# Rounding the last two weight pieces together, one slot later, in a fused attention and MLP kernel

## The chip, the core and the metric

The kernel runs on one core of a Trainium2 chip. The metric is device time in microseconds (us): the median of three runs is 1388.27 us, from 1384.64 to 1389.68. Five engines work side by side, each through its own instructions in order: TensorE (PE; its weight loads are shown as PEld), VectorE (DVE), ScalarE (ACT), GpSimd (POOL) and SyncE (SP, which here only starts transfers). They wait for each other through semaphores.

## The reference

Eight batches of eight heads attend over 576 positions of 64 channels, with a threshold on the scores. The result goes through a two-layer MLP with an exact gelu.

```python
scores = scale * np.matmul(q, k.transpose(0, 1, 3, 2))
thresh = np.max(scores, axis=-1, keepdims=True) - tau
scores = np.where(scores >= thresh, scores, -1000000000.0)
attn = np.exp(scores - np.max(scores, axis=-1, keepdims=True))
attn = attn / (np.sum(attn, axis=-1, keepdims=True) + 1e-09)
x = np.matmul(attn, v)          # then (B,H,S,D) -> (B*S, H*D): 4608 x 512
h = x @ w_in                    # 512 x 2048
out = (0.5 * h * (1.0 + erf(h / sqrt(2)))) @ w_out      # 2048 x 512
```

q, k, v and the result are 32-bit. The weights `moe_w_in` and `moe_w_out` arrive as 64-bit floats and have to be rounded to 32 bits on the core.

## The kernel before, in words

**Slots.** Two heads of a batch make a pair; there are 32 pairs. A pair's queries are cut into five chunks (`SLOTS`): four of 128 queries for each head, and one that holds the last 64 of both heads. One chunk of one pair is a slot, and the main loop (L832) goes over slots n = 0, 1, 2, ... The first batch's four pairs ("early", p = 0 to 3) take the first twenty slots: chunks 0 and 1 of each pair in n = 0 to 7, chunks 2, 3 and 4 in n = 8 to 19. So n = 17, 18 and 19 are chunks 2, 3 and 4 of pair 3, and n = 20 (`BATCH`) is the first slot of pair 4, where the later way of working begins.

**One slot.** PE computes the scores (L353). DVE takes the negated row maximum (L365), POOL the threshold (L366), ACT the exponential (L368), and DVE masks it by the threshold and sums each row (L384, "the mask" below). In an early slot the division and the turning of the probabilities are one matmul: DVE takes the reciprocal of the sums (L395), ACT scales an identity matrix by it (`diag`, L398), and PE multiplies the probabilities with that diagonal (L295), one slot later. ACT copies the turned tile from PSUM (L303, L314); for the last pair's chunk 4 DVE does so (L307, L319, `copy` at L305). After that, PE weighs v with them (L470).

**Between.** Into the same PE order `fill` puts steps of the MLP, block by block of 256 tokens: the first layer (L545) and the second (L559). How many steps a slot gets is planned by a cost per matmul (`goal`, `owed`), and a step is only placed once the weight pieces it needs are rounded in program order. Up to slot n = 19 the first layer's results are copied out ungelued (L512) and held; at n = 20 six of them go through gelu at once (L518). The last ten blocks go through a different scheme with fewer products (L679) at the end.

**Rounding the weights.** The weights are 32 pieces of 128 x 512 values: 16 of w_in, then 16 of w_out. `load_piece` brings a piece in two copies, `raw` and `shifted`, the second three bytes on. Pieces with an even number land in two buffers of the pool `xg` (seven buffers, shared with the MLP's input blocks `x_blk`). Pieces with an odd number land in a part of `turned_p` (L142), which the attention does not need before n = 20. Four pieces are loaded ahead: the load of piece k is issued when piece k - 4 is done. `conversions` rounds a piece with four DVE instructions and one of ACT: L168 (exponent bits), L169 on ACT (scaling them), L174 (mantissa bits), L176 (sign, needs L169) and L178 (product, the 32-bit value). It works one piece ahead: L168 and L169 of the next piece come before L174 of the one in hand.

`conversions` is a generator that yields a cost after each step, 2100 ns for a piece in all. The loop calls `convert(ns)` once a slot, after the mask and ahead of `diagonal` (the reciprocal and the diagonal): nothing at n = 0, 2000 ns at n = 1 and 2, 3800 ns up to n = 18, and from n = 19 on without limit (L896). Up to n = 18 that is 64,800 ns, enough for 30.9 pieces.

At n = 20 POOL clears parts of `pd_tail` and `turned_p` (L885), and the later slots write `turned_p` with DVE transposes (L431).

Of the kernel before, what the change touches and what calls it, by code (L numbers as in the profile page):

```python
# [18 lines left out]
def kernel(  # L19
# [82 lines left out]
    for t in sums:  # L102
# [17 lines left out]
    pieces = [(w_in_sb[c][:, f:f + PIECE], moe_w_in[c * P:(c + 1) * P, f:f + PIECE])  # L120
              for f in range(0, d_ff, PIECE) for c in range(N_DM)]
    pieces += [(w_out_sb[j][:, f:f + PIECE], moe_w_out[j * P:(j + 1) * P, f:f + PIECE])
               for j in range(N_DF) for f in range(0, d_model, PIECE)]
    wide = moe_w_in.dtype != FP32
    raws = []
    loaded = [0]
    converted = [0]

    def load_piece(eng=nc.gpsimd):
        if loaded[0] == len(pieces):  # L130
            return
        dst, src = pieces[loaded[0]]
        loaded[0] += 1
        if not wide:
            nc.sync.dma_start(dst, src)
            converted[0] += 1
            load_piece()
            return
        k = loaded[0] - 1
        if k % 2:  # L140

            room = pd[k // 2 % 2].bitcast(U32)  # L142
            raw, shifted = room[:, 0:2 * PIECE], room[:, 2 * PIECE:4 * PIECE]
        else:
            raw, shifted = (xg.tile([P, 2 * PIECE], U32, tag="x", name=s) for s in ("raw", "shifted"))
        eng.dma_start(raw, src.bitcast(U32))
        n = 8 * PIECE - 4
        eng.dma_start(shifted.bitcast(U8)[:, 0:n], src.bitcast(U8)[:, 3:3 + n])
        raws.append((dst, raw, shifted))

    def conversions():

        vec = nc.vector
        ahead = None  # L160
        while raws or ahead:
            piece = None
            if raws:
                dst, raw, shifted = raws.pop(0)
                hi = raw.rearrange("p (f w) -> p f w", w=2)[:, :, 1]
                top = shifted.rearrange("p (f w) -> p f w", w=2)[:, :, 0]
                power = gp.tile([P, PIECE], U32, tag="g", name="power")
                vec.tensor_scalar(power, hi, 0x7FF00000, None, op0=ALU.bitwise_and)  # L168
                nc.scalar.activation(power, power, AF.Relu, bias=rebias, scale=8.0)  # L169
                piece = dst, hi, top, dst.bitcast(U32), power  # L170
                yield 340
            if ahead:
                dst, hi, top, mant, power = ahead
                vec.tensor_scalar(mant, top, 0x0FFFFFFF, 0x10000000, op0=ALU.bitwise_and, op1=ALU.bitwise_or)  # L174
                yield 340
                vec.scalar_tensor_tensor(power, hi, 0x80000000, power, op0=ALU.bitwise_and, op1=ALU.bitwise_or)  # L176
                yield 720
                vec.scalar_tensor_tensor(dst, mant, 2.0 ** -28, power.bitcast(FP32), op0=ALU.mult, op1=ALU.mult)  # L178
                load_piece()
                converted[0] += 1  # L180
                yield 700
            ahead = piece
# [3 lines left out]
    def convert(ns):  # L186

        if conv["steps"] is None:
            conv["steps"] = conversions()
        conv["debt"] += ns  # L190
        while conv["debt"] > 0:
            took = next(conv["steps"], None)
            if took is None:
                return
            conv["debt"] -= took
# [600 lines left out]
    for _ in range(2):  # L796
        load_piece(nc.sync)
# [34 lines left out]
    for n in range(len(slots) + WEIGH + 1):  # L832
# [40 lines left out]
        if p < HP - 1 and i == 0:  # L873
            turn_qk_early(p + 1)
            if p == 0:
                load_early(3)
                load_v_early(2)
                load_v_early(3)
            if p < 2:
                load_piece()  # L880
# [70 lines left out]
```

## Time and profile before

| | |
|---|---|
| median of three runs | 1388.27 us (1384.64 to 1389.68) |
| profiled execution | 1389.68 us, of which the span of instructions is 1387.9 us |
| busy, share of the span | PE 98%, PEld 70%, DVE 64%, ACT 46%, POOL 31% |
| mean granted PE clock | 0.996 of full speed |
| slot n = 18, first maximum to reciprocal (DVE) | 135.96 to 143.66 us |
| slot n = 19, maximum to reciprocal (DVE) | 143.57 to 147.77 us |

Times in rows are us from the span's start. A timeline row has the start, the duration, the engine, the line, the operation with its output and inputs by name, the count of instructions that follow each other, and in brackets the idle time of the engine just before with what released it. A matmul of 32-bit numbers stands as two records, so "x20" is ten matmuls. The ends of matmuls are modelled, and rows can overlap by a little.

### The profile page before, as it was taken

The numbers are of one execution on the slowest core, as the hardware profiler recorded it, in microseconds if no ns is written. First come the engines' busy times: TensorE is split into PE (matmuls) and PEld (weight loads), VectorE is DVE, ScalarE is ACT, GpSimd is POOL, SyncE is SP. The second block draws the span as 40 slices with busy tenths as digits, with TensorE's granted clock in tenths as the row PEclk, the third lists the DMA queues.
The fourth block names the chain that finished last, engine by engine and source line by source line (L and its number), as shares of the span: only waits on it lengthen the run. The fifth ranks groups of instructions, "written<-read, shape, count | busy, mean of one in ns | idle before, by whom it ended". The sixth has DMA issues, their size and how long they took to land.

```text
span 1387.9 us, 20217 instructions
## 1 busy us (share of the span) xinstructions
PE 1361.0 (98%) x6728; PEld 968.8 (70%) x6728; DVE 892.8 (64%) x1738; ACT 640.1 (46%) x1161; POOL 434.4 (31%) x895
## 2 busy tenths in 40 slices
PE   8898999999999999999999999999999999999999
PEld 6676557467466466466476475588888888888887
DVE  5988777788888888888888888764142232241330
ACT  6766627447457458348367356241141240330420
POOL 4453254455555555554554551100000000000000
PEclk9999999999999999999999999999999999999999
DMA  8988266567777788787788776500000001001000
GB/s 274 279 296 275 56 150 160 130 160 175 161 168 182 156 189 179 157 197 176 157 199 177 162 181 129 116 0 8 23 1 23 23 1 46 16 0 53 8 9 23
DMA packets 215206, 169.19 MB, mean 122 GB/s; under 512 B 114288, under 2 KB 199600, under 8 KB 215104
## 3 DMA queue, kind: packets, MB, share of 16 engines
q1 hardware_dynamic: 191184, 112.84, 36.3%
q0 software_dynamic: 23488, 54.77, 12.9%
q8 instruction: 55, 0.90, 0.3%
q14 instruction: 47, 0.39, 0.1%
q10 hardware_dynamic: 432, 0.30, 0.1%
HBM read 72.73 MB, written 12.52 MB: 61 GB/s over the span
## 4 chain that ended last, share of the span: by engine, by line
PE 91%; DVE 5%; ACT 2%; issue 1%; DMA 1%; POOL 0%; DVEq 0%; ACTq 0%; POOLq 0%
PE bank L679 35%; PE o_ps L559 16%; PE hT L545 15%; PE sc L353 12%; PE xT L470 10%; DVE p L384 1%; DVE power L176 1%; PE tr L295 1%; ACT p L368 1%; PE tr L266 1%; DMA raw<-in_moe_w_out_dram 1%; ACT diag L398 1%; DVE power L168 1%; DVE w_out L178 1%; DVE w_in L178 1%
## 5 line engine op out<-in xcount | busy, mean ns | idle before, releaser
L368 ACT ACTIVATE p<-sc,nmx 128x576 f32<-128x576 f32 x288 | 201.9, 738 | 267.6 <-DVE nmx L365 267.4
L384 DVE SCALAR_TENSOR_TENSOR p<-sc,thr,p 128x576 f32<-128x576 f32 x288 | 225.3, 816 | 68.8 <-ACT p L368 67.3
L365 DVE TENSOR_REDUCE nmx<-sc 128x1 f32<-128x576 f32 x288 | 205.4, 750 | 65.8 <-PE sc L353 64.9
L545 PE MATMUL hT<-x,w_in 128*128 128x256 f32 x1024 | 241.1, 385 | 0.0
L559 PE MATMUL o_ps<-w_out,g 128*128 128x512 f32 x512 | 236.7, 603 | 0.0
L545 PEld LDWEIGHTS hT<-x,w_in 128*128 128x128 f32 x1024 | 189.5, 190 | 49.2 <-issue 23.5
L366 POOL TENSOR_SCALAR thr<-nmx,tau_eff 128x1 f32<-128x1 f32 x288 | 85.2, 296 | 393.3 <-DVE nmx L365 392.5
L559 PEld LDWEIGHTS o_ps<-w_out,g 128*128 128x128 f32 x512 | 93.0, 189 | 110.2 <-issue 108.6
L470 PE MATMUL xT<-pT,v 128*64 128x256 f32 (+1 forms) x1280 | 163.9, 409 | 0.4 <-issue 0.4
L353 PE MATMUL sc<-kT,qT 64*128 64x288 f32 x960 | 157.0, 431 | 2.0 <-DVE p L384 1.9
L431 DVE STREAM_TRANSPOSE turned_p<-p 128x1152 f32<-128x1152 f32 x112 | 154.4, 1379 | 3.9
L353 PEld LDWEIGHTS sc<-kT,qT 64*128 64x128 f32 x960 | 89.5, 187 | 75.0 <-issue 63.8
L470 PEld LDWEIGHTS xT<-pT,v 128*64 128x64 f32 x1280 | 89.0, 137 | 72.8 <-issue 14.0
L679 PE MATMUL bank<-x,w_in 128*128 128x256 f32 x480 | 116.7, 379 | 0.0
L679 PE MATMUL bank<-w_out,unit 128*128 128x256 f32 x520 | 115.5, 379 | 0.0
L223 POOL DMA_DIRECT2D v<-in_v_dram x208 | 111.2, 538 | 4.4 <-issue 2.4
L679 PEld LDWEIGHTS bank<-w_out,unit 128*128 128x128 f32 x520 | 98.8, 190 | 13.4
L679 PEld LDWEIGHTS bank<-x,w_in 128*128 128x128 f32 x480 | 91.2, 190 | 12.8 <-issue 0.5
L679 PE MATMUL bank<-v,unit 128*128 128x256 f32 x320 | 82.1, 379 | 0.0
L214 POOL DMA_DIRECT2D q<-in_q_dram x104 | 70.9, 687 | 9.8 <-issue 8.9
L679 PE MATMUL bank<-unit,turned_p 128*128 128x256 f32 x320 | 73.1, 379 | 0.0
L531 ACT ACT_TABLE_LOAD x56 | 71.8, 1283 | 1.0
(156 smaller groups left out, 1492.9 us busy)
## 6 DMA issues: line engine op xcount, KB each, us to landing
pT<-turned_p SPq DMA_DIRECT2D x448, 160.0 KB, 3.6
pT<-pd_tail SPq DMA_DIRECT2D x112, 80.0 KB, 3.1
q<-in_q_dram POOLq DMA_DIRECT2D x104, 72.0 KB, 3.3
k<-in_k_dram POOLq DMA_DIRECT2D x104, 72.0 KB, 3.2
inv<-turned SPq DMA_DIRECT2D x56, 128.0 KB, 3.9
v<-in_v_dram POOLq DMA_DIRECT2D x156, 40.0 KB, 3.2
x<-x SPq DMA_DIRECT2D x10, 512.0 KB, 4.8
raw<-in_moe_w_out_dram POOLq DMA_DIRECT2D x8, 512.0 KB, 4.1
```

Of the source, the lines that this page charges most:

```text
L223: eng.dma_start(t[r:P:4, e, 0:n, :], rows[:, r * KR:r * KR + n, :])
L353: nc.tensor.matmul(sc[e][:, h, 0:HALF], lhsT=lhsT, rhs=s["kT"][rows, at:at + HALF], start=True, stop=True)
L365: nc.vector.tensor_reduce(nmx[:, e:e + 1], sc, axis=AXIS.XY, op=ALU.max, negate=True)
L366: nc.gpsimd.tensor_scalar(thr[:, e:e + 1], nmx[:, e:e + 1], -1.0, tau_eff, op0=ALU.mult, op1=ALU.subtract)
L368: nc.scalar.activation(w[:, e * S:(e + 1) * S].rearrange("p (h s) -> p h s", h=2), sc, AF.Exp, bias=nmx[:, e:e + 1], scale=1.0)
L384: nc.vector.scalar_tensor_tensor(row, sc[e][:, :, 0:HALF], thr[:, e:e + 1], row, op0=ALU.is_ge, op1=ALU.mult, accum_out=den[e])
L431: nc.vector.transpose(turned_p[:, :, i // 2, 0:NB, i % 2 * Q:(i % 2 + 1) * Q], w.rearrange("p (e b i) -> p e b i", e=2, i=Q))
L470: nc.tensor.matmul(to, lhsT=s["v"][:, e, c, :], rhs=rhs, start=(c == 0), stop=(c == KR - 1))
L531: nc.scalar.activation(warm[:, 1:2], warm[:, 0:1], AF.Exp)
L545: nc.tensor.matmul(hT[:, j % 2, :], lhsT=w_in_sb[c][:, j * P:(j + 1) * P], rhs=x_blk[n][:, c, :], start=(c == 0), stop=(c == N_DM - 1))
L559: nc.tensor.matmul(o[:, 0:d_model], lhsT=g[j][:, m * P:(m + 1) * P], rhs=w_out_sb[j], start=(j == 0), stop=(j == N_DF - 1))
L679: nc.tensor.matmul(to, lhsT=l, rhs=r, start=start and k == 0, stop=k == len(pairs) - 1, skip_group_check=not start)
```

## The change

The two last pieces (`LATER = 2`, pieces 30 and 31) are held back. Once 30 pieces have been begun, `conversions` stops beginning new ones, finishes piece 29, and yields `None`, which ends the `convert` of that slot. That happens at n = 18, since 30 pieces cost 63,000 of the 64,800 ns. The call at n = 19 then rounds pieces 30 and 31. Before, n = 18 did L168 for pieces 30 and 31 and all of the rest of piece 30, and n = 19 only L174, L176 and L178 of piece 31. Also, piece 31 lands in two buffers of `xg`, as an even piece does, and no longer in `turned_p`.

The words that go with the change count slots from one (slot 19 is n = 18), and also speak of the rows in which the first queries and keys are loaded and of the tail copies on VectorE. Those stand in the kernel before already (L235 to L240, L305); the diff does not touch them.

```diff
     wide = moe_w_in.dtype != FP32
+    LATER = 2
     raws = []
...
         k = loaded[0] - 1
-        if k % 2:
+        if k % 2 and k < len(pieces) - LATER:
 
             room = pd[k // 2 % 2].bitcast(U32)
...
         ahead = None
+        begun = 0
         while raws or ahead:
+            if begun == len(pieces) - LATER and not ahead:
+                yield None
+                begun += 1
             piece = None
-            if raws:
+            if raws and begun != len(pieces) - LATER:
+                begun += 1
                 dst, raw, shifted = raws.pop(0)
```

## The prediction

> **What bounds the kernel now.** I read the page first, then the chain of waits, then the timeline of each engine where the change acts.
>
> ```profile
> PE 1361.0 (98%) x6728; PEld 968.8 (70%) x6728; DVE 892.8 (64%) x1738; ACT 640.1 (46%) x1161; POOL 434.4 (31%) x895
> PE 91%; DVE 5%; ACT 2%; issue 1%; DMA 1%; POOL 0%; DVEq 0%; ACTq 0%; POOLq 0%
> ```
>
> TensorE (PE) is busy 98% of the span, and 91% of the chain that ended last is PE. About 27 us of PE idle time exist at all (1387.9 - 1361.0). The PE timeline shows some 20 us of it before 170 us; after that come only 0.71 us at 621.8, 0.42 at 892.4, five gaps of 0.5 us, one per pair of blocks at the end (DVE L729 ahead of L679), and the last store (3 us). None of these is slack against an earlier delay: each is a wait on something that PE itself has just started. So whatever delays PE before 170 us pushes everything behind it, and nothing later gives it back.
>
> The change acts at 134 to 152 us. These are the VectorE (DVE) rows there, in columns start, duration, engine, line, operation, count, and in brackets the idle time before with its releaser:
>
> ```profile
> 139.07 0.42 DVE L168 TENSOR_SCALAR power<-raw 128x512 uint32<-128x512 uint32 x1
> 139.41 0.42 DVE L174 TENSOR_SCALAR w_out<-turned_p 128x512 uint32<-128x512 uint32 x1
> ...
> 142.16 0.69 DVE L176 SCALAR_TENSOR_TENSOR power<-raw,power 128x512 uint32<-128x512 uint32 x1 [0.34 <-ACT power L169]
> 142.89 0.69 DVE L178 SCALAR_TENSOR_TENSOR w_out<-w_out,power 128x512 f32<-128x512 uint32 x1
> 143.50 0.16 DVE L395 RECIPROCAL den<-den 128x2 f32<-128x2 f32 x1
> ...
> 145.20 0.82 DVE L384 SCALAR_TENSOR_TENSOR p<-sc,thr,p 128x576 f32<-128x576 f32 x1 [0.89 <-ACT p L368]
> 145.94 0.08 DVE L384 DVE_READ_ACCUMULATOR p<-sc,thr,p 128x1 f32 x1
> 145.94 0.42 DVE L174 TENSOR_SCALAR w_out<-turned_p 128x512 uint32<-128x512 uint32 x1
> 146.28 0.68 DVE L176 SCALAR_TENSOR_TENSOR power<-turned_p,power 128x512 uint32<-128x512 uint32 x1
> 147.00 0.69 DVE L178 SCALAR_TENSOR_TENSOR w_out<-w_out,power 128x512 f32<-128x512 uint32 x1
> 147.61 0.16 DVE L395 RECIPROCAL den<-den 128x1 f32<-128x1 f32 x1
> ```
>
> The first reciprocal closes slot n=18, the second slot n=19. Each feeds the diagonal on ScalarE (ACT, L398) with which PE turns that slot's probabilities (L295). ACT and PE at the same place:
>
> ```profile
> 146.78 0.27 ACT L314 COPY pT<-tr 128x128 f32<-128x128 f32 x1
> 147.86 0.40 ACT L398 ACTIVATE diag<-ident,den 128x128 f32<-128x128 f32 x1 [0.81 <-DVE den L395]
> 144.25 2.37 PE L295 MATMUL tr<-diag,p 128*128 128x128 f32 x20
> 146.56 1.24 PE L353 MATMUL sc<-kT,qT 64*128 64x288 f32 x8
> 148.31 1.52 PE L295 MATMUL tr<-diag,p 128*128 128x128 f32 x10 [0.51 <-ACT diag L398]
> ```
>
> What to see: PE starts the turn of n=18 at 144.25 with no idle time before it. It starts the turn of n=19 after 0.51 us of waiting for the diagonal. So the reciprocal of n=19 is on the path, and that of n=18 is not: it has cover of PE's own work from 140.7 on.
>
> **The change part by part.** I compared the order of instructions on each engine. All counts are equal. PE and SP issue the same instructions in the same order. Only these differ.
>
> (a) DVE, slot n=18: five of the eight rounding instructions go: L168 for pieces 30 and 31, then L174, L176 and L178 for piece 30. From 139.07 there remain L174, L176, L178 of piece 29, at starts 0.34, 0.72 and 0.61 apart. The reciprocal starts near 140.75 instead of 143.50. The gain for PE is nothing: the cover is the row at 144.25, which waits for nobody; PE has been at work without a gap since the turn at 138.67. Were the diagonal (done in part by 144.1) the true releaser there, at most some 0.2 us could be won, as the hT matmuls in front start at 142.09 and ten of them take 2.3.
>
> (b) DVE and ACT, slot n=19: the eight instructions after the mask (L384) are now both L168, then L174, L176, L178 of piece 30 and the same of piece 31, all ahead of the reciprocal. The two ACT instructions L169 are moved too: in ACT's order they stand behind the copies L303, L303, L314 of the turn of n=18. This is a new wait. L176 of piece 30 needs the first L169, which needs L314, which needs PE's turn, fixed at 144.25 to 146.6. The mask ends earlier than now, but L176 cannot follow. In the old slot n=18 the same sequence stands: L314 starts at 141.24, L176 at 142.16, 0.92 later. So L176 of piece 30 starts at 146.78 + 0.92 = 147.70. From there by the starts in the rows: L178 +0.72, L174 +0.61, L176 +0.34, L178 +0.72, reciprocal +0.61, together 3.00: the reciprocal starts at 150.70 instead of 147.61, **3.1 us** later. Behind it on DVE stands the maximum of n=20 (L365), behind that on ACT the exponentials and the held gelus; on PE the turn of n=19 and, in order, all the rest. PE is idle from 147.80 to 151.40, that is 3.6 us in place of 0.51. What could catch up: DVE's next rows wait for PE's scores (2.96 us at 156.41, 3.89 at 164.91), and PE's one later gap there (1.59 at 167.52) hangs on scores, maximum, exponential and mask in a row, which all move along. Nothing is caught up.
>
> (c) POOL: the two transfers of piece 31 go to two buffers that piece 28 leaves, not to turned_p. They wait for L174 and L176 of piece 28 (done by 134.65 and 135.24) instead of L176 of piece 27 (133.2). They are issued 1.2 us later, until 135.9; the next instruction on POOL is thr at 136.88. Landings of such transfers took up to 9.8 us (raw) and 10.8 (shifted): 144.5 and 146.1 against needs at 145.0 and 149.0. Nothing. The later memsets of turned_p and x buffers go to memory that is free sooner or as soon: nothing, as L431 at 151.07 waits for none of it now.
>
> (d) The clock. A gap on PE can cost more than its length here:
>
> ```profile
> 22.02 3.44 PE L295 MATMUL tr<-diag,p 128*128 128x128 f32 x20 [1.82 <-ACT diag L398]
> 37.06 2.42 PE L295 MATMUL tr<-diag,p 128*128 128x128 f32 x20 [1.89 <-ACT diag L398]
> 51.68 4.41 PE L295 MATMUL tr<-diag,p 128*128 128x128 f32 x20 [2.72 <-ACT diag L398]
> 24.00:26.00 2.00, 2.00 (x16) 1.77 (x17) 1.97 (x6) 0.89 (x3) 1.28 (x3) 0.50 0.89 261
> 51.00:57.00 6.00, 5.32 (x24) 4.62 (x26) 5.57 (x12) 4.21 (x9) 3.11 (x8) 0.50 0.96 321
> ```
>
> The last two rows are the busy time in two stretches, with the granted clock as the third number from the end: 0.50. By stretches of 1 us it was at half from 23.1 to 26.5 (3.4 us) and from 50.4 to 57.2 (twice that), behind gaps of 1.82 and 2.72; gaps of 1.89, 2.10 and 1.80 (at 37.1, 65.8, 138.7) had none. One such window cost 3.44 - 2.42 = 1.0 in the turn and 0.6 in the transposes behind (1.68 against 1.04 for the same sixteen), so 1.6 us; the double one 2.0 + 0.6 = 2.6. Bounds for the new gap of 3.6: 0 and 2.6. I take 1.6, one window: the new gap is longer than any that lost the clock, and the work behind it (twenty hT matmul records, 4.58 us) is PE's own.
>
> The Trainium skill ("TensorE: Matmul & The Clock Gate", section "Why this matters for your kernels") asks for no PE-idle gaps over about 3 us and says that one idle window brings the half clock; this trace lost it after less, 1.82 us. The page's section "What's actually happening" makes the window 3.4 us and free-running: read strictly, a gap of 3.6 us would hold a whole one in few phases, and the sum would be 3.1 alone; by the rows above it is 4.7.
>
> **Sum.** 3.1 + 1.6 = +4.7 us, 0.34%. The profiled execution took 1389.68 us (span 1387.9 and 1.8 around it), 1.4 over the median of 1388.27; against the median the forecast is 1393.0. That is within 0.5% (6.9 us), about what a measurement of this kernel can tell from no change: the three runs of before lie 5.0 apart.
>
> **The rivals.**
> - *Gap without clock* (chance 0.24): 3.1 alone, 1391.4. For it: the three gaps near 2 us that lost nothing. Against: none of them is as long.
> - *Two windows* (0.15): 3.1 + 2.6, 1394.0. For it: the gap of 2.72 drew two.
> - *Slower by over 0.5%* (0.22): the slow clock is met by the next gap. PE's 1.59 at 167.52 comes while the clock has only just recovered and draws a third window: 3.1 + 2.6 + 1.6 = 7.3, 1395.6. It decides from the third slow window on. Against: that gap lost nothing in the run before.
> - *Not slower* (0.06; half of it over 0.5% faster by spread of runs): the diagonal was the true releaser at 144.25 and the L169 pair gets ahead of the turn's copies. Then 0.2 and the 0.51 are won, 1387.6. Against: ACT's order is fixed. The gaps that remain in this stretch are too small for 6.9 us.
> - The change does less than its words, where it could: counted from one, slots 19 and 20 are n=18 and n=19, and piece 30 moves whole. So it acts.
>
> **How the numbers follow.** The likeliest case (0.33) is gap and one window, 1393.0. Its own spread is that of the runs, about 2 us each way. The range runs from no change seen (1388) to the third window and some spread (1397.5). Over 0.5% slower begins at 1395.2: rival three, 0.22 with its tails. Faster by over 0.5%: 0.03. The rest, 0.75, is within.
>
> **What would show it.** On PE the turn of n=19 starts about 3 us later, with 3.5 to 3.7 us idle before it, put down to the diagonal; on DVE L176 of piece 30 waits some 2 us for ACT L169. The granted clock reads 0.50 for about 3.4 us soon after. The turn of n=18 stays where it is. If the reciprocal of n=19 comes at the same time as now, step (b) is wrong; if later PE gaps shrink by as much, the shift was caught up.

## The result, and the profile after

The changed kernel takes 1394.65 us (median of four runs, 1392.37 to 1395.37), against 1388.42 us for the kernel before (1384.64 to 1389.68). The ratio is 1.0047, with a 95% interval of 1.0024 to 1.0069: 6.2 us slower, by medians. The forecast was 1393.0, inside a range from 1388 to 1397.5. The profiled execution of the changed kernel took 1395.02 us, with a span of 1393.2 us; that is 5.3 us longer than the span before (1387.9). Times further on are medians of runs in the usual state, and each ratio is against the kernel before run beside it; one run of the kernel with three idle instructions, 1993.47 us at a mean granted clock of 0.656, is left out.

Lines of the changed kernel stand six further on than those of the kernel before (L168 is now L174, L169 is L175, L295 is L301, and so on). The timeline of DVE, in slot n=19:

```profile
144.93 0.76 DVE L174 TENSOR_SCALAR power<-raw 128x512 uint32<-128x512 uint32 x2
145.60 0.42 DVE L180 TENSOR_SCALAR w_out<-shifted 128x512 uint32<-128x512 uint32 x1
147.90 0.69 DVE L182 SCALAR_TENSOR_TENSOR power<-raw,power 128x512 uint32<-128x512 uint32 x1 [1.88 <-ACT power L175]
...
150.90 0.16 DVE L401 RECIPROCAL den<-den 128x1 f32<-128x1 f32 x1
```

L182 (before: L176) of piece 30 waits 1.88 us for ACT's scaling, which stands behind the copies of PE's turn. The reciprocal comes at 150.90, where it came at 147.61. PE in the same stretch and behind it:

```profile
144.51 2.32 PE L301 MATMUL tr<-diag,p 128*128 128x128 f32 x20
146.76 1.24 PE L359 MATMUL sc<-kT,qT 64*128 64x288 f32 x8
151.60 1.54 PE L301 MATMUL tr<-diag,p 128*128 128x128 f32 x10 [3.61 <-ACT diag L404]
153.08 6.20 PE L551 MATMUL hT<-x,w_in 128*128 128x256 f32 x20
...
172.45 2.74 PE L359 MATMUL sc<-kT,qT 64*128 64x288 f32 x8 [1.58 <-DVE p L390]
175.12 5.41 PE L565 MATMUL o_ps<-w_out,g 128*128 128x512 f32 x10
...
627.57 1.21 PE L359 MATMUL sc<-kT,q_tail 128*128 128x288 f32 x4
```

The gap ahead of the turn of n=19 has grown from 0.51 to 3.61 us. The twenty hT records behind it take 6.20 us. Further on, the gap of 1.58 us ahead of a set of scores is as long as it was (1.59), but the scores and the second-layer steps behind it are slow as well. The last row had a gap of 0.71 us ahead of it before; now it has none. Busy time by stretches, with the granted clock third from the end:

```profile
153.00:156.00 3.00, 3.00 (x9) 2.37 (x8) 2.96 (x7) 2.97 (x5) 0.52 (x4) 0.50 0.01 3
174.00:176.00 2.00, 2.00 (x5) 0.83 (x3) 1.99 (x5) 0.00 (x0) 0.67 (x2) 0.50 0.80 198
```

PE ran at half clock from 153.0 to 156.4 and from 173.4 to 176.9. For comparison, the same places in the PE timeline of the kernel before:

```profile
149.76 4.58 PE L545 MATMUL hT<-x,w_in 128*128 128x256 f32 x20
...
167.52 1.94 PE L353 MATMUL sc<-kT,qT 64*128 64x288 f32 x8 [1.59 <-DVE p L384]
...
621.81 1.21 PE L353 MATMUL sc<-kT,q_tail 128*128 128x288 f32 x4 [0.71 <-DVE p L384]
```

So the 5.3 us can be followed along PE. The lag of the changed kernel, start against start of the same row, is

| place on PE | lag, us | what was added |
|---|---|---|
| turn of n=17 (138.67, now 138.93) | 0.3 | present before the change acts |
| turn of n=19 (148.31, now 151.60) | 3.3 | 3.0 to 3.1: the gap |
| scores behind the 1.58 us gap (167.52, now 172.45) | 4.9 | 1.6: half clock on hT (6.20 - 4.58) |
| behind the slow scores and steps (173.79, now 180.36) | 6.6 | 1.65: (2.74 - 1.94) + (5.41 - 4.56) |
| chunk 4 at 621.81, now 627.57 | 5.8 | -0.8: that gap closed (0.71 to 0) |
| turned values at 892.37, now 897.70 | 5.3 | -0.4: a second small gap and the row ahead of it got shorter |
| end of the span | 5.3 | |

### The profile page after: what moved, and what is told of

Same layout as the page of the kernel before. It is cut to its first block, busy times and chain, and to the rows that moved or that the text cites. A ratio compares the mean times of both kernels' runs of the same rounds, so it can differ in the third digit from the quotient of the medians.

```text
span 1393.2 us, 20218 instructions
## 1 busy us (share of the span) xinstructions
PE 1364.6 (98%) x6728; PEld 971.9 (70%) x6728; DVE 892.8 (64%) x1738; ACT 639.9 (46%) x1161; POOL 434.3 (31%) x895
## 4 chain that ended last, share of the span: by engine, by line
PE 90%; DVE 5%; ACT 2%; DMA 1%; issue 1%; SPq 0%; POOL 0%; DVEq 0%; ACTq 0%; POOLq 0%
PE bank L685 35%; PE o_ps L565 16%; PE hT L551 15%; PE sc L359 12%; PE xT L476 10%; DVE p L390 1%; DVE power L182 1%; PE tr L301 1%; ACT p L374 1%; DVE w_out L184 1%; ACT diag L404 1%; DVE power L174 1%; DMA turned_p<-in_moe_w_in_dram 1%; DVE w_in L184 0%; PE tr L272 0%
```

## The experiments

The theory was: the loss is the rounding of two whole pieces ahead of the reciprocal of n=19, plus what the gap does to PE's clock. The rivals were the new place of piece 31, and that delay or clock cost nothing on the path.

**One half of the change alone.** First the buffers without the hold, then the hold without the buffers:

```diff
+    LATER = 2
...
-        if k % 2:
+        if k % 2 and k < len(pieces) - LATER:
```

> The kernel before with one half of the change alone: piece 31 lands in two buffers of the pool xg; nothing is held back. Theory: no cost, 1387.5 to 1389.5 us, PE gap ahead of the turn of n=19 about 0.5 us. Rival (the buffers or the transfer 1.2 us later cost it): 1393 us or more.

Measured: 1388.94 us, ratio to the kernel before 1.0005 (0.9993 to 1.0017).

```diff
-        if k % 2 and k < len(pieces) - LATER:
+        if k % 2:
```

(in the changed kernel)

> The changed kernel with the other half alone: pieces 30 and 31 are held back to n=19, piece 31 lands in turned_p as before. Theory: the whole loss, 1393.5 to 1395.5 us, with the gap of 3.6 us on PE. Rival (the buffers cost it): 1388 to 1389 us.

Measured: 1394.42 us, ratio 1.0039 (1.0024 to 1.0054). The turn of n=19 on PE, first with the buffers alone, then with the hold alone:

```profile
149.38 1.52 PE L296 MATMUL tr<-diag,p 128*128 128x128 f32 x10 [0.51 <-ACT diag L399]
```

```profile
149.91 2.70 PE L301 MATMUL tr<-diag,p 128*128 128x128 f32 x10 [3.60 <-ACT diag L404]
```

Both came as expected. The loss lies in the hold; the buffers, and the transfer of piece 31 that they put off, cost nothing that the interval shows (at most 0.17%).

**A delay with nothing else moved.** In the kernel before, k idle DVE instructions stand between the rounding and the reciprocal of n=19:

```diff
+        if n == BATCH - 1:
+            same = w_out_sb[N_DF - 1].bitcast(U32)
+            for _ in range(k):        # 3, 6 or 9
+                nc.vector.tensor_scalar(same, same, 0, None, op0=ALU.bitwise_or)
         if early:
             diagonal(p, i)
```

> As with nine, but three idle DVE instructions, 1.02 us. PE gap ahead of the turn of n=19 about 1.5 us. Theory: a delay of up to 1.25 us is given back by the gaps of 0.71 at 622 us and 0.42 at 892 us, as in the changed kernel, and a gap of 1.5 us seldom loses the clock: 1388 to 1389.5 us. Rival (every delay lasts to the end, or the clock is lost): 1389.5 to 1391.5 us.

> As with nine, but six idle DVE instructions, 2.04 us. PE gap about 2.5 us. Theory: 0.8 us that is not given back, and one half-clock window (1.6 us) in most executions, as behind the gaps of 2.72 and 2.58 us: 1389 to 1392.5 us, between the runs with three and with nine. Rival (the time follows the delay alone): 1389.3 us and no half clock.

> The kernel before, with nine idle DVE instructions (an OR with zero of a rounded piece, 0.34 us apart, 3.06 us in all) between the rounding and the reciprocal of n=19. Nothing else is moved. Theory (the changed kernel's loss is this delay and what it draws behind it): the same time as the changed kernel, 1393 to 1395.5 us, PE gap 3.6 us, a half clock of 3.4 us behind it. Rival (the shorter slot n=18 or the moved L169 matter too): 1388 to 1390 us, or over 1397.

The idle instructions came 0.46 us apart and not 0.34 (each works on the output of the one ahead of it). So the PE gaps were 1.90, 3.29 and 4.67 us, as the three profiles show (three, six, nine):

```profile
149.22 2.69 PE L295 MATMUL tr<-diag,p 128*128 128x128 f32 x10 [1.90 <-ACT diag L398]
```

```profile
148.86 2.69 PE L295 MATMUL tr<-diag,p 128*128 128x128 f32 x10 [3.29 <-ACT diag L398]
```

```profile
151.16 2.70 PE L295 MATMUL tr<-diag,p 128*128 128x128 f32 x10 [4.67 <-ACT diag L398]
```

| | gap on PE | time, us | ratio to the kernel before |
|---|---|---|---|
| kernel before | 0.51 | 1388.60 | 1 |
| three | 1.90 | 1391.54 | 1.0021 (1.0009 to 1.0034) |
| six | 3.29 | 1394.61 | 1.0037 (1.0024 to 1.0049) |
| nine | 4.67 | 1395.50 | 1.0042 (1.0028 to 1.0057) |

The gap of the changed kernel, 3.61 us, lies between six and nine, and so does its time within the intervals. A bare delay of the reciprocal thus gives the loss; the shorter slot n=18 and the moved ACT instructions are not needed for it. With three and with six instructions the expectations on the time were missed: I expected up to 1389.5 and up to 1392.5 us. The delays were longer than meant, and the clock cost more. With three I had counted on small gaps further on to absorb a delay of 1 us; a delay of 1.4 us cost 2.9 us by the ratio: in that profile PE was at half clock for 6.8 us from 149.1, and again for 3.4 us from 173.0. With six the two stretches took 6.8 us each, from 147.4 and from 171.3.

**The gap filled with matmuls.** The changed kernel, with work for PE while it waits:

```diff
+        if n == BATCH:
+            spare = ps.tile([P, 512], FP32, tag="mm", name="spare")
+            for _ in range(12):
+                nc.tensor.matmul(spare[:, 0:P], lhsT=ident, rhs=ident, start=True, stop=True)
         gelus(0)
```

> The changed kernel with twelve more matmuls of the identity with itself (some 2.9 us, result unused) on PE between the scores of n=20 and the turn of n=19, where PE is idle for 3.61 us. The wait for the diagonal stays as long. Theory (the gap costs its length, and the half clock behind it adds 1.6 us or more): no half clock at 153 to 156 us, PE's idle time there 0.5 to 0.9 us, the turn of n=19 still near 151.6 us; time 1.6 us less than the changed kernel if the window at 173 us stays, 3.3 less if it goes too: 1391 to 1393 us. Rival (the clock costs nothing, as other engines set the end of this stretch): 1394 to 1395 us.

Measured: 1393.13 us, ratio 1.0034 (1.0021 to 1.0047). Its PE timeline:

```profile
147.84 2.94 PE L850 MATMUL spare<-ident 128*128 128x128 f32 x24
151.52 1.52 PE L301 MATMUL tr<-diag,p 128*128 128x128 f32 x10 [0.73 <-ACT diag L404]
152.97 4.58 PE L551 MATMUL hT<-x,w_in 128*128 128x256 f32 x20
```

The turn starts as late as in the changed kernel, but the clock stays full and the hT records take 4.58 us again. In this profile no half clock came after 71 us, and its span is 1391.4 us, 3.5 more than before: the gap alone, without the clock. The median is just over the expected band, and run times do not set it apart from the hold alone (1.0039). So the profile shows the clock's part, and the run times bound it only loosely.

**Where the rounding may stand.** In the changed kernel, the reciprocal of n=19 goes ahead of the rounding:

```diff
+        if n == BATCH - 1:
+            diagonal(p, i)
         convert(0 if n == 0 else 2000 if n < 3 else 3800 if n < BATCH - 1 else 1e9)
-        if early:
+        if early and n != BATCH - 1:
             diagonal(p, i)
```

> The changed kernel, with the reciprocal and the diagonal of slot n=19 ahead of the rounding instead of behind it. Theory (what costs is that the reciprocal of n=19 stands behind two whole pieces): the gap of 3.61 us on PE ahead of the turn of n=19 is gone, to under 0.3 us, and no half clock follows at 153 to 156 us. The maximum of n=20 stays late (near 151 us), and with it the held gelus, so up to 1.5 us may appear as a wait at the first L559 step. Time 1388 to 1390 us. Rival (the two new buffers, or the later transfer of piece 31, cost it): 1394 to 1395 us as the changed kernel.

Measured: 1391.29 us, ratio 1.0019 (1.0006 to 1.0031). The gap ahead of the turn is gone, but another one has come:

```profile
155.61 1.38 PE L565 MATMUL o_ps<-w_out,g 128*128 128x512 f32 x2 [2.62 <-DVE pT L313]
```

It is 2.62 us where I allowed up to 1.5, the time is over the expected 1388 to 1390 us, and the releaser is not the held gelus that I named. The first second-layer step needs a PSUM bank which the tail copies on DVE (L313 here, L307 before) empty. Those stand behind the mask and the maximum of n=20, and these behind the rounding. A half clock followed this gap too, from 156.3. Two pieces in n=19 are in the way twice.

Then the hold was made one slot longer, by a second `yield None`, so that the pieces are rounded in n=20 behind the tail copies:

> The changed kernel with the two last pieces held back by one slot more, to n=20, where the rounding stands behind the mask of n=20 and the tail copies. Theory (what costs is rounding ahead of the reciprocal and the maximum of n=20): no PE gap ahead of the turn of n=19 (under 0.3 us), no gap at the first L559 step as in the run with the diagonal first, since the maximum of n=20 follows at once. DVE had 2.96 us of idle time before the maximum of n=21, and the rounding takes 4.4 us, so that maximum may come some 2 us later; its mask is needed by PE two slots on. Time 1387 to 1390 us. Rival (the rounding costs as much wherever DVE does it): 1393 us or more.

Measured: 1389.52 us, ratio 1.0001 (0.9990 to 1.0012). No gap is left at the turn or at the first second-layer step. The price is one gap grown from 1.58 to 3.25 us:

```profile
167.95 3.00 PE L360 MATMUL sc<-kT,qT 64*128 64x288 f32 x8 [3.25 <-DVE p L391]
```

The same rounding costs nothing measurable one slot on (the interval runs from -1.4 to 1.7 us). What cost was its place. The grown gap is not free in the profile, though: PE was at half clock for 6.8 us behind it, from 167.5, and DVE's masks (L384 before, L391 here) went from 0.4 us behind the kernel before to 3.1 us. The times do not show it.

**The reciprocal early everywhere.** The waits for the diagonal at n=19 are one of nine in the kernel before. In this version of the kernel before, every early slot takes its reciprocal after 30% of its rounding:

```diff
-        convert(0 if n == 0 else 2000 if n < 3 else 3800 if n < BATCH - 1 else 1e9)
+        ns = 0 if n == 0 else 2000 if n < 3 else 3800 if n < BATCH - 1 else 1e9
         if early:
+            convert(min(ns, 3800) * 0.3)
             diagonal(p, i)
+        convert(ns - min(ns, 3800) * 0.3 if early else ns)
```

> The kernel before, with the reciprocal and diagonal of every early slot after the first 30% of the slot's rounding instead of after all of it. Theory: PE's waits for the diagonal in the first 150 us (12.2 us in nine) shrink, with the half-clock windows behind them; DVE is 85 to 90% busy there, so only its idle time can be won: 1383 to 1387 us. Rival 1 (DVE alone sets the pace of these slots): 1387.5 to 1389.5 us. Rival 2 (the reciprocal now waits for POOL's sum and DVE loses that time in each slot): 1390 us or more.

Measured: 1384.94 us, ratio 0.9972 (0.9959 to 0.9985): faster than the kernel before, and than the changed one. PE's waits for the diagonal in the first 200 us (total, times, longest), in the kernel before and in this one:

```profile
PE tr L295 <- ACT diag L398: 12.2, 9, 2.7
```

```profile
PE tr L295 <- ACT diag L398: 1.1, 3, 0.7
```

Of the 11 us that went, some 4 arrived, since PE now waits for the mask instead (7.2 us in five waits, against 2.2 in three).

The change on top of this order, with the pieces in n=19 and in n=20. An early slot now calls `convert` twice, and each `None` ends one call, so the pieces come in n=19 behind the diagonal with two `yield None`, and in n=20 with three:

> The changed kernel with the reciprocal and diagonal of every early slot ahead of most of its rounding (in n=19 ahead of all of it). Theory: the order with the early diagonal gains what it gained on the kernel before (0.28%, 1384.9 us), and the change on top of it costs what remained when only n=19 had its diagonal first (1391.3 against 1388.6, 2.7 us), since the two pieces still stand ahead of the maximum of n=20 and of the tail copies, whose bank in PSUM the first L559 step needs: a PE gap of about 2.6 us there, 1386.5 to 1389 us. Rival (with the diagonal early everywhere the change costs nothing): 1384 to 1386 us.

> As the run before it, with the two pieces held back to n=20, behind the tail copies. Theory: no PE gap at the turn of n=19 nor at the first L559 step; only the gap ahead of the scores two slots later grows (1.58 to about 3.2 us, as in the run with n=20 alone), so no gain over the early diagonal alone: 1384 to 1387 us. Rival (the pieces were still in the way at n=19 with the early diagonal): 1382 to 1384 us.

Measured: 1388.72 us, ratio 1.0008 (0.9995 to 1.0021), and 1388.06 us, ratio 1.0005 (0.9995 to 1.0015); the kernel before beside them took 1387.52 us. The profiles, in this order:

```profile
151.69 1.10 PE L566 MATMUL o_ps<-w_out,g 128*128 128x512 f32 x2 [2.62 <-DVE pT L314]
```

```profile
166.00 2.99 PE L361 MATMUL sc<-kT,qT 64*128 64x288 f32 x8 [3.23 <-DVE p L392]
```

Both gaps are where they were foretold. In n=19 the pieces take back what the early reciprocal wins, as expected. In n=20 they were expected to leave the gain (up to 1387 us), and did not. In its profile the gap of 3.23 us drew a half clock of 6.8 us, from 166.5. That may be the reason but is not shown to be: with the pieces in n=20 alone the same gap drew the same half clock, and the times showed no loss.

**The clock in the early slots.** The kernel before, with seven matmuls ahead of the turn in four slots where PE waits for the diagonal:

```diff
+        if n in (2, 4, 6, 8):
+            spare = ps.tile([P, 512], FP32, tag="mm", name="spare")
+            for _ in range(7):
+                nc.tensor.matmul(spare[:, 0:P], lhsT=ident, rhs=ident, start=True, stop=True)
         if last and last[0] < EARLY and last[1] < NC:
```

> The kernel before with seven matmuls of the identity with itself (1.7 us, result unused) on PE ahead of the turn in slots n=2, 4, 6 and 8, where PE waits 1.8 to 2.7 us for the diagonal. Theory (the half clock follows gaps of that length and costs time): fewer half-clock windows between 20 and 75 us (none or one, against three in the profile before), the time in the fast part of the range of the kernel before: 1384 to 1387 us. Rival (DVE sets the pace there and the half clock costs nothing): 1388 to 1389.5 us; if the seven matmuls themselves delay the turn, 1389.5 us or more.

Measured: 1389.71 us, ratio 1.0006 (0.9994 to 1.0018). The half clock between 20 and 75 us was gone (three windows before, none in this profile; the mean clock of its runs lies from 0.996 to 1.000). The time did not move (the kernel before beside it took 1389.53 us), so the expectation is missed. The seven matmuls did not hold up the turns to any visible degree: in three of the four slots the turn still waits for the diagonal behind them (0.56, 1.25 and 1.57 us), and in the fourth it starts as early as the masks ahead of it do.

That does not show that the early half clock costs nothing. DVE's masks (L384) in this profile, start against start of the kernel before, came 1.4 us early ahead of the first of the seven-matmul groups, 3.0 us early behind the place of the first window (23.1 us), which is the 1.6 us worked out for one window, and 2.2 us early from 59 to 173 us. So 0.8 us of it was left. Then a new half clock came, from 165.9 to 172.7 us, behind a gap that lost nothing in the kernel before:

```profile
165.33 2.99 PE L353 MATMUL sc<-kT,qT 64*128 64x288 f32 x8 [1.58 <-DVE p L384]
168.26 6.77 PE L559 MATMUL o_ps<-w_out,g 128*128 128x512 f32 x10
```

These rows took 1.94 and 4.56 us before. The 3.2 us put the masks 1.0 us behind. So the run does not settle what the early windows are worth. A cleaner case is in the profile of the changed kernel: it has a window from 67.6 to 71.1 us that the kernel before has not, and the lag of the masks is 0.83 us ahead of it and 0.82 behind it, though the turn there took 3.49 us and not 2.42:

```profile
66.61 3.49 PE L301 MATMUL tr<-diag,p 128*128 128x128 f32 x20 [2.58 <-ACT diag L404]
```

There, where PE waits for DVE, a half clock cost nothing. At 153 us, where DVE waits for PE, it cost 1.6 us.

## Why the prediction was right, and where it was not

- **(a), slot n=18 gives nothing:** right. The reciprocal came 2.5 us earlier (141.00 against 143.50) and PE's turn of n=18 did not move ahead (144.51 against 144.25, with the lag of 0.3 that was there already).
- **(b), 3.1 us at the turn of n=19:** right to 0.1 us. L182 of piece 30 was worked out to wait about 2 us for ACT, and waited 1.88; the PE gap was worked out as 3.6, and was 3.61. The delay and the hold alone show that this is the cause of the loss. How much of it is the clock's rests on the profiles.
- **(c), the buffers cost nothing:** right, shown by the buffers alone. The transfer of piece 31 did come later on POOL, at 135.20 and not 133.48: 1.7 us, where 1.2 had been worked out.
- **(d), the clock, one window of 1.6 us:** the first window measured 1.62. The step that failed is the count. A second window came behind the gap of 1.58 us, 1.65 us more, where the kernel before had lost nothing. The third rival named this place and its price, but only as a third window behind a double one. In five profiles with a half clock behind the turn of n=19 (the changed kernel, the hold alone and the three delays), all five had it again there; of the other seven profiles with that gap at 1.58 or 1.59 us, one had it. What the six have in common is where the gap falls in time (last section). Over runs, the mean granted clock fell from 0.9947 (93 runs of the kernel before, beside the experiments) to 0.9922 (the four of the changed one): some 0.0024 of 1390 us is 3.4 us of clock, as much as two windows of 3.41 us at half. The profiles differ by three, of which the one at 67.6 us cost nothing.
- **"Nothing later gives it back":** wrong. The gaps of 0.71 at 621.8 and 0.42 at 892.4 gave back 1.2 us. I had argued that such gaps wait for what PE itself has just started. What closes such a gap stays open. With the filling matmuls, the one at 622 us rose to 1.04 us; with the half clock it closed. But it closed also with the buffers alone, where no half clock came between 72 us and the end of the work, and there the lag fell by 0.9 us.
- **The sum:** 3.1 + 1.6 + 1.65 - 1.2 is 5.2, against 5.3 in the profiles, of which 0.3 stood there before the change acts. The forecast of 4.7 was near partly by luck: its two errors, a window too few and 1.2 us that it did not expect back, stood on opposite sides. By medians the loss was 6.2 us.
- **The rule on gaps** in the Trainium skill ("TensorE: Matmul & The Clock Gate", section "Why this matters for your kernels") asks for no PE-idle gaps above about 3 us. Here that was too mild. The clock was lost behind gaps of 1.58 us (changed kernel) and 1.90 us (three idle instructions).

## What to carry to other kernels

Work that is put off lands ahead of something else on the same engine: before moving it, list what stands behind its new place, and prefer a place where that engine waits anyway (here one slot later, behind the copies that free a bank). A short result which another engine waits for, such as a reciprocal, belongs ahead of long work nobody waits for. Where PE sets the pace, a pause cost its length and often the clock behind it (1.6 us for a window); where PE waits for another engine, a half clock may cost nothing (0 at 67.6 us here), but that has to be read from the lag at that place.

## What the runs showed of the hardware

- The half clock came in stretches of 3.41 us or twice that, in all profiles (a last one, behind PE's last matmul, is cut off by the end). The starts of the half clocks within a profile lie whole multiples of 3.413 us apart, as on a grid that runs through (in the changed kernel 23.26, 50.57, 67.64, 152.97 and 173.45).
- Gap length alone did not decide: gaps of 1.66 to 1.85 us ahead of the turn of n=17 lost nothing in eleven profiles, while one of 1.58 us lost it in the changed kernel and not in the kernel before. Where the gap falls on that grid went with it: in the changed kernel it lies whole in one stretch (170.86 to 172.45, in 170.04 to 173.45), in the kernel before the grid cuts it at 166.47 (165.93 to 167.52). In the twelve profiles with this gap at 1.58 or 1.59 us it lay whole in six, which all lost the clock, and was cut in six, of which none did. No run moved the gap alone to test this. Ahead of the turn of n=17 it was not enough: in the kernel before the 1.80 us lie whole in one stretch (136.87 to 138.67, in 135.75 to 139.17) and lost nothing. What decides in general stays open.
- The 93 runs of the kernel before spread from 1385 to 1393 us, and go with the mean granted clock: on average 1386.4 us at 0.996 (26 runs), 1388.3 at 0.995 (20), 1389.3 at 0.994 (35), 1390.6 at 0.993 (10). That the clock is the cause is not shown: in the ten runs with the early half clock cleared the time does not follow it (1385.66 us at 0.999, 1390.27 at 1.000).
- DVE instructions of 128x512 that rewrite each other's output came 0.46 us apart (nine in 4.12 us); those on separate tiles 0.34 (139.07 to 139.41 before).
